# Turning the last row group of block 0 by DMA instead of on TensorE, with a fourth feature computed meanwhile

## The chip, the cores and the metric

The kernel runs on one core of one Trainium2 chip. The metric is the device time of one execution in microseconds (us); the figure before the change is the median of three runs. The profile is of one more execution, whose own time is given beside its span below.

## The reference

The input is x, 2048 rows of 512 features in bf16. The rows are normalised, and two branches of the normalised rows are added to x:

```
xn  = layernorm(x)                                   # over the 512 features
ssm : Bu = xn @ B_bar^T;  h[t] = Lam_bar * h[t-1] + Bu[t]   (complex, 512 states)
      y  = 2 * Re(h @ C^T) + xn * Dskip
glu : out = (silu(xn @ w1) * (xn @ w3)) @ w2         # 1792 hidden features
result = x + y + out
```

B_bar and Lam_bar are made from the small parameters Lambda_re, Lambda_im and log_dt (512 values each).

## The kernel before, in words

The 2048 rows are cut into four blocks of 512 rows, and a block into four row groups of 128 rows (groups 0 to 3). The 1792 hidden features are cut into 14 features of 128 (here a "feature" f is such a group of 128 columns of w1 and w3). TensorE needs the normalised rows turned, with the 512 input features on the partitions: that is the tile `xnT` of a block, 128 partitions by 4 by 512. For feature f of a block, `glu_mm` (L372) adds four matmuls into one PSUM bank for w1 (`g_ps`) and four into another for w3 (`u_ps`), each 128 by 512. ScalarE then takes the bank of w1 through silu (L388, `sl16`) and copies that of w3 (L390, `up16`); VectorE multiplies the two into `hgT` (L397). There are eight PSUM banks.

The order of the work on every engine is the order in which the program text issues it: the schedule is written by hand. Only the side work of VectorE is taken from a queue (`push`, `drain`) between features, in a fixed order.

Blocks 1 to 3 are turned by transposing DMAs that SyncE issues (L232). Block 0, at the start, is turned on TensorE: `turn(c, ...)` issues four 128 by 128 transposes for row group c (L251) into a PSUM tile, and `put` copies them into `xnT` on ScalarE (L256) or VectorE (L258). To keep TensorE at work while the rows arrive and are normalised, `ahead(...)` computes features 0, 1 and 2 on those row groups that are already turned, 128 or 256 rows at a time; their six banks are `begun`. The other two banks hold `xt_a` and `xt_b`, in which the transposes land. The small parameters lie in the tile `prm` and are transposed by one matmul (L544); `par_cols` copies the result out on ScalarE (L271), takes an exponential (L273), and GpSimd makes small columns of them. `glu_up` then runs over all 14 features of block 0; for a feature in `begun` it does only the rows of group 3 (`ts = slice(TBLK - P, TBLK)`).

Around the change, block 0's start runs like this. VectorE normalises group 2 (`normed(2)`, L192); TensorE does half of w3's products for groups 0 and 1, transposes group 2, does the other half, transposes `prm`, and does features 0 for group 2; VectorE has meanwhile copied group 2 (`put(2)`, L258) and normalised group 3 (L192). TensorE then transposes group 3, and does features 1 and 2 of group 2 while VectorE copies group 3 out (L258). ScalarE computes `r_col` (L549), loads the table of silu (L550) and begins with feature 0.

The DMAs of the weights go through SyncE's ring in this order: w1 and w3 for features 0 to 3, then 4 to 7, then the rows of block 1, then w1 and w3 for features 8 to 13 (L95, L117), `dskip_row` (L119), the eight transposing DMAs that load `bt` (L103, for the state-space branch), the rows of block 2, and later the four turns of block 1 (L232). ScalarE's own ring carried only the small parameters and the rows of groups 2 and 3 of block 0, at the very start (L109, L77).

Of the kernel before, what the change touches and what calls it, by code (L numbers as in the profile page):

```python
# [16 lines left out]
P = 128  # L17
# [3 lines left out]
def kernel(  # L21
# [24 lines left out]
    nc = tc.nc  # L46
# [8 lines left out]
    NDT = D // P  # L55
# [14 lines left out]
    def ps_tile(name):  # L70
        return psum.tile([P, 512], FP32, name=name, tag="ps")
# [10 lines left out]
    w1_sb = const.tile([P, NDT, F], BF16, name="w1_sb")  # L82
    w3_sb = const.tile([P, NDT, F], BF16, name="w3_sb")
# [4 lines left out]
    H = NDT // 2  # L88
# [56 lines left out]
    begun = [(ps_tile("g_ps"), ps_tile("u_ps")) for _ in range(3)]  # L145
# [13 lines left out]
    xnTs = [None] * NBLK  # L159
# [28 lines left out]
    def normed(c, parts=1):  # L188
        xn = work.tile([P, D], BF16, name="xn", bufs=8)
        for i in range(parts):  # L190
            ds = slice(i * D // parts, (i + 1) * D // parts)
            nc.vector.tensor_scalar(out=xn[:, ds], in0=x_blk[c // CPB][:, c % CPB, ds], scalar1=mv_all[:, c, 0:1],  # L192
                                    scalar2=rstd_all[:, c:c + 1], op0=ALU.subtract, op1=ALU.mult)
        return xn
# [49 lines left out]
    xt_a = psum.tile([P, 2 * NDT, P], BF16, name="xt_ps", tag="ps")  # L244
    xt_b = psum.tile([P, 2 * NDT, P], BF16, name="xt_ps", tag="ps")
    pprm = xt_a[:, NDT]
    xn0 = xns_of[0] = {}

    def turn(c, pxt, d0=0, d1=NDT):
        for dt in range(d0, d1):  # L250
            nc.tensor.transpose(out=pxt[:, dt - d0, :], in_=xn0[c][:, dt * P:(dt + 1) * P], identity=ident)  # L251

    def put(c, pxt, eng, d0=0, d1=NDT):
        dst = xnTs[0][:, d0:d1, c * P:(c + 1) * P]
        if eng is nc.scalar:
            nc.scalar.activation(out=dst, in_=pxt, func=ACT.Copy)  # L256
        else:
            nc.vector.tensor_copy(out=dst, in_=pxt)  # L258
# [10 lines left out]
    def par_cols():  # L269
        prmc = const.tile([P, 3 * NPT], FP32, name="prmc")  # L270
        nc.scalar.activation(out=prmc, in_=pprm[:, :3 * NPT], func=ACT.Copy)  # L271
        col["lre"], col["lim"], col["ldt"] = (prmc[:, i * NPT:(i + 1) * NPT] for i in range(3))
        nc.scalar.activation(out=c4("dt"), in_=col["ldt"], func=ACT.Exp)  # L273
        nc.gpsimd.tensor_tensor(out=c4("kr"), in0=col["dt"], in1=col["lre"], op=ALU.mult)
        nc.gpsimd.tensor_tensor(out=c4("ki"), in0=col["dt"], in1=col["lim"], op=ALU.mult)
        nc.gpsimd.tensor_scalar(out=c4("turn"), in0=col["ki"], scalar1=float(1.0 / (2.0 * np.pi)), scalar2=None,
                                op0=ALU.mult)
        tt = nc.gpsimd.tensor_tensor
        tt(out=c4("den"), in0=col["lre"], in1=col["lre"], op=ALU.mult)
        tt(out=c4("d2"), in0=col["lim"], in1=col["lim"], op=ALU.mult)  # L280
        tt(out=col["den"], in0=col["den"], in1=col["d2"], op=ALU.add)
# [87 lines left out]
    def glu_mm(b, f, w_sb, ps, ts, dts=range(NDT), joins=False):  # L369

        for dt in dts:
            nc.tensor.matmul(out=ps[:, ts], lhsT=w_sb[:, dt, f * P:(f + 1) * P], rhs=xnTs[b][:, dt, ts],  # L372
                             start=(dt == 0 and not joins), stop=(dt == NDT - 1))
# [128 lines left out]
    def ahead(w_sbs, fs, c, n=1, dts=range(NDT), joins=False):  # L502
        for f in fs:
            for w_sb in w_sbs:
                glu_mm(0, f, w_sb, begun[f][w_sb is w3_sb], slice(c * P, (c + n) * P), dts, joins)

    t1 = [ps[:, :P].bitcast(BF16).rearrange("p (t c) -> p t c", c=P) for ps in begun[2]]
    ta, tb, t2, t3 = xt_a[:, :H], xt_b[:, :H], xt_b[:, NDT:], xt_a[:, :NDT]

    stats(0)  # L510
    aggr(0)
# [19 lines left out]
    B3 = (0, 1, 2)  # L531
    lo, hi = range(H), range(H, NDT)
# [5 lines left out]
    rstd_act(3, 4)  # L538
    ahead((w3_sb,), B3, 0, 2, lo)
    turn(2, t2)  # L540
    put(2, t2, nc.vector)
    xn0[3] = normed(3)
    ahead((w3_sb,), B3, 0, 2, hi)
    nc.tensor.transpose(out=pprm, in_=prm, identity=ident)  # L544
    par_cols()
    ahead((w1_sb, w3_sb), (0,), 2)
    turn(3, t3)
    put(3, t3, nc.vector)
    nc.scalar.activation(out=r_col, in_=col["kr"], func=ACT.Exp)  # L549
    nc.scalar.preload_act_table_set("silu_and_others")  # L550
    ahead((w1_sb, w3_sb), (1, 2), 2)

    push([(3.2, par_turns), (0.2, par_recip)])
    push([(0.0, lambda: for_act.extend(par_trig()))])
# [53 lines left out]
```

## Time and profile before

| what | value |
|---|---|
| median of 3 runs | 211.85 us (211.66 to 211.96) |
| the profiled execution's own time | 212.11 us |
| its span in the profile | 210.3 us |
| TensorE (PE) busy | 206.6 us, 98% of the span |
| VectorE (DVE) busy | 173.5 us, 82% |
| ScalarE (ACT) busy | 93.4 us, 44% |
| granted TensorE clock | 1.0 |
| SyncE's DMA ring (q1) | 13.24 MB |
| ScalarE's DMA ring (q10) | 0.27 MB |

The span runs from the first to the last instruction in the trace; the 1.8 us by which the execution's own time is longer lie outside it. All times below are counted from the start of the span. PEld is TensorE's weight load, which overlaps the matmuls. "SPq" and "ACTq" rows are DMA issues: their length is the time in which the issuing engine's sequencer is taken up, not the time of the transfer.

### The profile page before, as it was taken

The page shows a single profiled execution, that of the slowest core. Times are in us where ns is not written, and L with a number is a line of the kernel's source. Part 1 is how long each engine was busy: PE and PEld are TensorE (multiplying, and loading weights), DVE is VectorE, ACT ScalarE, POOL GpSimd, SP SyncE. Part 2 cuts the span into 40 slices and gives each one's busy share as a digit, 9 for nine tenths or more (in the row PEclk, how much of TensorE's full clock was granted, in tenths as well). Part 3 has the DMA queues.
Part 4 walks back from the last instruction along what each step waited for, and adds up shares of the span by engine and source line. Part 5 has one row for each costly group of instructions (what it writes and reads, how often), then busy time and mean ns, then how long its engine had stood idle before and what let it go on. Part 6 is the DMA issues. An engine that isn't in the chain of part 4 may idle for free.

```text
span 210.3 us, 2878 instructions
## 1 busy us (share of the span) xinstructions
PE 206.6 (98%) x1036; PEld 97.7 (46%) x1036; DVE 173.5 (82%) x346; ACT 93.4 (44%) x167; POOL 6.0 (3%) x27
## 2 busy tenths in 40 slices
PE   8999999999999999999999999999999999999994
PEld 3864444444444444444444444444444444444453
DVE  4699989989999999999999999999999999121111
ACT  3599967666666200066666600036666620000000
POOL 2010320000000000000000000000000000000000
PEclk9999999999999999999999999999999999999999
DMA  5999599944000000000004200100000000000110
GB/s 165 294 366 219 109 178 325 217 106 100 0 3 0 0 25 25 28 26 0 0 0 77 28 1 24 50 25 5 0 0 0 0 3 25 27 25 25 34 44 25
DMA packets 25014, 13.69 MB, mean 65 GB/s; under 512 B 15912, under 2 KB 25000, under 8 KB 25000
## 3 DMA queue, kind: packets, MB, share of 16 engines
q1 hardware_dynamic: 24704, 13.24, 26.1%
q10 hardware_dynamic: 296, 0.27, 0.4%
q8 instruction: 8, 0.13, 0.3%
q14 instruction: 6, 0.05, 0.1%
HBM read 7.74 MB, written 2.10 MB: 47 GB/s over the span
## 4 chain that ended last, share of the span: by engine, by line
PE 96%; DMA 2%; SPq 0%; DVE 0%; issue 0%
PE g_ps L372 23%; PE u_ps L372 23%; PE y_ps L488 23%; PE y_ps L493 13%; PE bu_ps L411 13%; DMA w_sb<-in_B_w_dram 2%; SPq L77 0%; PE xt_ps L251 0%; DVE o L498 0%; PE xt_ps L544 0%
## 5 line engine op out<-in xcount | busy, mean ns | idle before, releaser
L372 PEld LDWEIGHTS <-w_sb 128*128 128x128 bf16 x502 | 46.4, 98 | 50.6 <-DMA w_sb<-in_B_w_dram 0.6
L372 PE MATMUL g_ps<-xnT,w_sb 128*128 128x512 bf16 (+2 forms) x254 | 58.2, 354 | 0.3 <-DMA w_sb<-in_B_w_dram 0.3
L372 PE MATMUL u_ps<-xnT,w_sb 128*128 128x512 bf16 (+2 forms) x248 | 58.4, 358 | 0.0
L488 PE MATMUL y_ps<-w_sb,hgT 128*128 128x512 bf16 (+2 forms) x238 | 51.2, 366 | 0.0
L390 ACT ACTIVATE up<-u_ps 128x512 bf16<-128x512 f32 x56 | 34.0, 607 | 14.9 <-PE u_ps L372 14.9
L413 ACT ACTIVATE u<-bu_ps 128x512 bf16<-128x512 f32 x32 | 19.1, 597 | 46.3 <-PE bu_ps L411 46.3
L388 ACT ACTIVATE sl<-g_ps 128x512 bf16<-128x512 f32 x56 | 34.0, 608 | 9.9 <-PE g_ps L372 9.2
L445 DVE TENSOR_TENSOR_SCAN ab<-r_col,h,ab 128x256 bf16<-128x256 f32 x56 | 37.7, 733 | 0.2
L488 PEld LDWEIGHTS <-hgT 128*128 128x128 bf16 x238 | 22.8, 98 | 25.9
L498 DVE TENSOR_TENSOR o<-y_ps,x_blk 128x512 bf16<-128x512 f32 (+2 forms) x17 | 11.1, 654 | 24.3 <-PE y_ps L493 24.3
L493 PE MATMUL y_ps<-ct,h 128*128 128x512 bf16 (+2 forms) x136 | 30.4, 366 | 0.0
L411 PE MATMUL bu_ps<-xnT,bt 128*128 128x512 bf16 x128 | 28.1, 379 | 0.0
L397 DVE TENSOR_TENSOR hgT<-sl,up 128x512 bf16<-128x512 bf16 x56 | 22.9, 414 | 2.1 <-ACT up L390 2.1
L493 PEld LDWEIGHTS <-h 128*128 128x128 bf16 x136 | 13.0, 98 | 14.7
L411 PEld LDWEIGHTS <-bt 128*128 128x128 bf16 x128 | 12.5, 98 | 15.1
L164 DVE BATCH_NORM_STATS2 stats<-x_blk 128x6 f32<-128x512 bf16 x16 | 10.6, 675 | 2.5 <-DMA x_blk<-in_A_x_dram 2.5
L454 DVE TENSOR_TENSOR ab<-ab,tab_s 128x2048 bf16<-128x2048 bf16 x8 | 9.8, 1222 | 0.2
L450 DVE TENSOR_TENSOR ab<-ab,tab_c 128x2048 bf16<-128x2048 bf16 x8 | 9.8, 1222 | 0.1
L427 DVE TENSOR_TENSOR ab<-u,tab_x 128x2048 bf16<-128x2048 bf16 x8 | 9.7, 1219 | 0.0
L430 DVE TENSOR_TENSOR ab<-u,tab_y 128x2048 bf16<-128x2048 bf16 x8 | 9.7, 1218 | 0.0
L201 DVE TENSOR_TENSOR x_blk<-xd,x_blk 128x512 bf16<-128x512 bf16 x16 | 6.8, 426 | 0.5
L200 DVE TENSOR_TENSOR xd<-xn,dskip_row 128x512 bf16<-128x512 bf16 x16 | 6.7, 418 | 0.0
(76 smaller groups left out, 81.3 us busy)
## 6 DMA issues: line engine op xcount, KB each, us to landing
out_dram<-o SPq DMA_DIRECT2D x15, 128.0 KB, 1.7
w_sb<-in_B_w_dram SPq DMA_DIRECT2D x1, 1792.0 KB, 9.3
x_blk<-in_A_x_dram SPq DMA_DIRECT2D x3, 512.0 KB, 6.3
w_sb<-in_B_w_dram SPq DMA_DIRECT2D x2, 768.0 KB, 7.8
w_sb<-in_B_w_dram SPq DMA_DIRECT2D x4, 256.0 KB, 5.0
w_sb<-in_B_w_dram SPq DMA_DIRECT2D x2, 512.0 KB, 4.1
x_blk<-in_A_x_dram SPq DMA_DIRECT2D x2, 128.0 KB, 2.2
x_blk<-in_A_x_dram ACTq DMA_DIRECT2D x1, 256.0 KB, 4.7
```

Source lines behind the costliest of these rows:

```text
L164: nc.vector.bn_stats(out=sums[c], in_=x_blk[c // CPB][:, c % CPB, :])
L372: nc.tensor.matmul(out=ps[:, ts], lhsT=w_sb[:, dt, f * P:(f + 1) * P], rhs=xnTs[b][:, dt, ts], start=(dt == 0 and not joins), stop=(dt == ...
L388: nc.scalar.activation(out=sl16, in_=g_ps, func=ACT.Silu)
L390: nc.scalar.activation(out=up16, in_=u_ps, func=ACT.Copy)
L397: nc.vector.tensor_tensor(out=hg[b][:, f, :], in0=sl16, in1=up16, op=ALU.mult)
L411: nc.tensor.matmul(out=u_ps, lhsT=bt[ri][:, dt, pt * P:(pt + 1) * P], rhs=xnTs[b][:, dt, :], start=(dt == 0), stop=(dt == NDT - 1))
L413: nc.scalar.activation(out=u16[:, :, pt, ri, :], in_=u_ps.rearrange("p (s t) -> p s t", s=NSB), func=ACT.Copy)
L445: nc.vector.tensor_tensor_scan(out=a[:, pt, 2 * ri + 1, :], data0=r_b, data1=a[:, pt, 2 * ri, :], initial=init, op0=ALU.mult, op1=ALU.add)
L450: nc.vector.tensor_tensor(out=a[:, :, 0::2, :], in0=a[:, :, 1::2, :], in1=tab_b("c"), op=ALU.mult)
L488: nc.tensor.matmul(out=y_ps[:, ds], lhsT=hg[b][:, f, cl * P:(cl + 1) * P], rhs=w2_sb[:, f, ds], start=(f == 0), stop=False)
L493: nc.tensor.matmul(out=y_ps[:, ds], lhsT=h_tiles[i][:, pt, ri, h_ts], rhs=ct[ri][:, pt, ds], start=False, stop=(pt == NPT - 1 and ri == 1))
L498: nc.vector.tensor_tensor(out=o16[:, ds], in0=y_ps[:, ds], in1=x_blk[b][:, cl, ds], op=ALU.add)
```

## The change: a transposing DMA on ScalarE's ring, and feature 3 started early

Group 3 of block 0 is no longer turned on TensorE. After `par_cols`, ScalarE issues one transposing DMA that writes the columns of group 3 into `xnT` straight from the normalised rows in SBUF. The four transposes (L251) and VectorE's copy (L258) of that group are gone. `normed(3)` stands ahead of `put(2)` on VectorE, and the transpose of `prm` and `par_cols` stand ahead of the second half of w3's products. A fourth pair of banks is taken for feature 3 (the banks that held `xt_a` and `xt_b`), and features 0 to 3 are done for groups 0 to 2 before `glu_up` begins.

```diff
-    ta, tb, t2, t3 = xt_a[:, :H], xt_b[:, :H], xt_b[:, NDT:], xt_a[:, :NDT]
+    ta, tb, t2 = xt_a[:, :H], xt_b[:, :H], xt_b[:, NDT:]
...
     turn(2, t2)
+    xn0[3] = normed(3)
     put(2, t2, nc.vector)
-    xn0[3] = normed(3)
-    ahead((w3_sb,), B3, 0, 2, hi)
     nc.tensor.transpose(out=pprm, in_=prm, identity=ident)
     par_cols()
-    ahead((w1_sb, w3_sb), (0,), 2)
-    turn(3, t3)
-    put(3, t3, nc.vector)
+    nc.scalar.dma_start_transpose(out=xnTs[0][:, :, 3 * P:], in_=xn0[3])
+    ahead((w3_sb,), B3, 0, 2, hi)
+    begun.append((ps_tile("g_ps"), ps_tile("u_ps")))
+    ahead((w1_sb,), (3,), 0, 2)
+    ahead((w1_sb, w3_sb), B3, 2)
+    ahead((w3_sb,), (3,), 0, 2)
+    ahead((w1_sb, w3_sb), (3,), 2)
     nc.scalar.activation(out=r_col, in_=col["kr"], func=ACT.Exp)
     nc.scalar.preload_act_table_set("silu_and_others")
-    ahead((w1_sb, w3_sb), (1, 2), 2)
```

In the compiled order of the changed program, the first `bt` DMA on SyncE waits for the new DMA to land, and the first matmul of `glu_up` (feature 0, group 3) waits for it too. The order of all other instructions on the five engines is as before.

## The prediction

> **What bounds the kernel now.** I read the page first: engine totals, then the chain of work that ended last.
>
> ```profile
> PE 206.6 (98%) x1036; PEld 97.7 (46%) x1036; DVE 173.5 (82%) x346; ACT 93.4 (44%) x167; POOL 6.0 (3%) x27
> ...
> PE 96%; DMA 2%; SPq 0%; DVE 0%; issue 0%
> ```
>
> TensorE is the bound. In the timeline its matmuls run back to back from 6.48 us to the end; after 6.48 no start is later than the matmul before it explains. So only two things can change the time: the number of columns TensorE streams, and a new wait of TensorE. Every microsecond of such a wait goes to the end, one for one, because no later gap can absorb it.
>
> Next the timeline around the change, 8 to 12.4 us (start, length, engine, line, operation, tiles).
>
> ```profile
> 8.46 0.20 ACT L172 ACTIVATE rstd_all<-rstd_all 128x1 f32<-128x1 f32 x1
> 8.49 0.39 PE L251 MATMUL xt_ps<-ident,xn 128*128 128x128 bf16 x4
> ...
> 8.72 0.82 PE L372 MATMUL u_ps<-xnT,w_sb 128*128 128x256 bf16 x6
> 8.92 0.42 DVE L258 COPY xnT<-xt_ps 128x512 bf16<-128x512 bf16 x1 [0.73 <-PE xt_ps L251]
> 9.26 0.40 DVE L192 TENSOR_SCALAR xn<-x_blk,mv_all,rstd_all 128x512 bf16<-128x512 bf16 x1
> ...
> 9.37 0.22 PE L544 MATMUL xt_ps<-ident,prm 128*128 128x128 bf16 x1
> ...
> 9.63 0.18 ACT L271 ACTIVATE prmc<-xt_ps 128x12 f32<-128x12 bf16 x1 [0.97 <-PE xt_ps L544]
> ...
> 9.84 0.20 ACT L273 ACTIVATE c_dt<-prmc 128x4 f32<-128x4 f32 x1
> 9.88 0.39 PE L251 MATMUL xt_ps<-ident,xn 128*128 128x128 bf16 x4
> ...
> 10.59 1.28 ACT L550 ACT_TABLE_LOAD   x1
> ...
> 10.84 1.94 SPq L103 DMA_TRANSPOSE bt<-in_A_B_re_dram  x1
> ```
>
> The row of four transposes at 9.88 is what the change removes; the next PE row starts at 10.10, so they cost 0.22 us, 0.056 each. The six 256-row matmuls from 8.72 to 9.37 start 0.109 apart; the 512-row ones from 12.33 on start 0.216 apart.
>
> Last, what a transposing DMA of this very shape takes when the DMA engines are otherwise idle (block 2's turns, 46 to 53 us), and what the rings did. The issue durations are minimum/median/maximum in ns.
>
> ```profile
> L232 SPq DMA_TRANSPOSE xnT<-xn x4: 1212/1216/1221, 46.4 to 50.3; - x4
> ...
> DMA to landing us min/median/max: 2.3/2.3/2.4
> ```
>
> The same kind of issue while the weights were still streaming:
>
> ```profile
> L103 SPq DMA_TRANSPOSE bt<-in_A_B_re_dram x4: 1587/1869/2677, 10.8 to 17.4; - x4
> ```
>
> Rings in three windows: 46 to 53, 9 to 12, and 3.75 to 5 us (packets, MB, share of 16 engines' time).
>
> ```profile
> q1 hardware_dynamic: 2720, 0.66, 41.6%
> ```
> ```profile
> q1 hardware_dynamic: 1120, 1.11, 107.6%
> ```
> ```profile
> q1 hardware_dynamic: 233, 0.23, 54.6%
> q10 hardware_dynamic: 195, 0.19, 42.3%
> ```
>
> The first window is five transposing DMAs: 544 packets each, 34 on each engine, at 0.416 x 16 x 7000 / 2720 = 17 ns. The second is the weights: all 16 engines full, 1.076 x 16 x 3000 / 1120 = 46 ns a packet. The third is the one stretch in which ScalarE's ring and SyncE's ring both had work: they got 195 and 233 packets, close to one for one.
>
> **The change part by part: TensorE's own work.** Removed: 4 transposes x 0.056 = 0.22 us. Feature 3 was 8 matmuls of 512 rows, 8 x 0.216 = 1.73; it is now 8 of 256 and 16 of 128 rows, 8 x 0.109 + 16 x 0.056 = 1.77, so +0.04. Net -0.18 us: the whole possible gain, 0.09% of the time. About 0.2%, here 0.42 us, is what a measurement of this kernel can tell from no change.
>
> **The cover.** After group 2's transposes end their slots at 8.72, TensorE has this to do before it needs group 3: `prm` 0.06; six matmuls of 256 rows, 0.65; four of 256, 0.44; 24 of 128, 1.34; four of 256, 0.44; eight of 128, 0.45. It comes to the waiting matmul at 12.09 us. Its other inputs are in time: `put(2)` moves behind `normed(3)`, to 9.13 to 9.55, and is needed at 9.86; the bank of `xt_a` is read by L271 by 9.16 and needed at 9.43; the weights of feature 3 came with those of features 0 to 2.
>
> **When the DMA is issued.** `normed(3)` needs L172, done at 8.66: with 0.40 it ends at 9.10. The transpose of `prm` comes 0.65 earlier, at 8.72, so L271 runs at 8.98 and L273 at 9.19 to 9.39. The issue stands behind both on ScalarE: about 9.3 (between 9.2, if only L273's dispatch holds it, and 9.4).
>
> **When it lands.** Idle engines: 9.3 + 2.3 = 11.6, half a microsecond inside the cover. But it runs at 10 to 13 us, where the windows show 16 engines full with weights. If its 34 packets on each engine alternate with weight packets, as the two rings did at 3.75 to 5 us, its data takes 34 x (17 + 46) = 2.1 us in place of 34 x 17 = 0.6: 1.55 us more. It lands at 9.3 + 2.3 + 1.55 = 13.15. The trace holds no transposing DMA against another ring's backlog, so both sides are bounded: below by 11.6, above by the slowest `bt` issue, 2.68 in place of 1.21, which adds 1.46 and gives 14.6. I take 13.15, because the window of two rings is the nearest row; the other transfer on ScalarE's ring beside weights, 256 KB of rows, took 4.7 us from issue to landing, which would give 14.0. Start of the waiting matmul: 13.2 with 0.05 from landing to start, as at 6.43 to 6.48. TensorE then stands still for 13.2 - 12.09 = 1.11 us.
>
> The Trainium skill speaks against the move: "VectorE: DVE Perf Modes", section "The three transpose paths", gives 1309 ns for a 128 by 128 block by DMA against 390 ns on TensorE. As an estimate from that page, four such blocks in a row are 5.2 us, a landing at 14.5 and a time of 214.1. The trace differs on both sides: 2.3 us for four blocks in one DMA, 0.056 for one in TensorE's stream.
>
> **What waits behind it.** On ScalarE the issue holds back L549 and the table load (1.28), then silu of feature 0. With 1.2 to 2.7 us of issue the table is in at 12.0 to 13.5; feature 0 is complete at 13.65, so TensorE's wait hides it. Feature 4 needs feature 0's `g_ps` bank back: silu ends at about 14.4, TensorE is there at 15.0. Without TensorE's wait the table is in at 12.0 against 12.5 for feature 0, still hidden. VectorE loses the 0.42 copy, in idle time. On SyncE `dskip_row` (L119) stays ahead, but the first `bt` issue waits for the landing, 10.84 to 13.15, with the rest of SyncE's queue behind it: the other `bt` DMAs, block 2's rows, block 1's turns. At most 2.3 us of delay: the last `bt` landed at 25.6 and is first used at 31.1; block 1's turns landed at 31.3 and are first used at 38.4. The weights of features 4 to 7 had landed by 12.2, and the new packets take 0.6 us of each engine; w3's are used from 14.9 on. All of this costs nothing.
>
> **The sum.** -0.18 + 1.11 = +0.93 us. On the profiled execution, 210.3 + 1.8 around it = 212.11, that is 213.04; on the median, which lies 0.26 lower, 212.8.
>
> **Rivals.** *Covered (0.20).* ScalarE's ring is its own, with nothing ahead of it, and the DMA lands near the idle 2.3 us. It decides at 12.04: earlier, and TensorE never waits and keeps the whole -0.18, 211.67; up to 12.2 it still isn't slower, and up to 12.65 it is within 0.2%. For it: the ring carries nothing else then, and a lull in DMA share (0.69 in 7 to 9 us) lies just before. Against it: 1.07 in 9 to 11 and 1.10 in 11 to 13, and the 4.7 us of ScalarE's other load. "DMA: Bandwidth & Descriptors", section "Issuing engines are not separate DMA queues" in the Trainium skill, says that DMAs of all issuers run on the same 16 engines and interleave; the two rings at 3.75 to 5 us agree.
>
> *Slow issue as well (0.22).* The issue itself is stretched as the `bt` ones were, to 1.6 to 2.7 us, on top of the shared engines: landing at 13.55 to 14.6; with the wait counted as above, 213.2 to 214.2. For it: four of four such issues between 10.8 and 19 were long, and SyncE issues `dskip_row` in 1.31 at that moment. Against it: they went into a ring with its own backlog.
>
> *Blocks in series (0.04).* The four blocks of the DMA go one after another, each with the 1.1 us from end of issue to landing: 1.2 + 4 x 1.1 = 5.6, landing at 14.9, 214.5. The 2.3 us row speaks against it. The Trainium skill's 1309 ns, above, is of this kind.
>
> **How the numbers follow.** Forecast 0.52, and slower with the last two: 0.78. Covered or nearly, within 0.2%: 0.20. Faster by over 0.2%: 0.02, since -0.18 is all there is, and only scatter could add to it. The range goes from 211.6 (covered, with the runs' scatter of 0.1) to 214.3 (the slowest issue, with the same scatter).
>
> **What would show it.** Right: on PE a gap of about 1.1 us before L372's first 128-row matmul of group 3, near 12.1, ended by the DMA `xnT<-xn`; that DMA 3.9 us from issue to landing; ring q10 beside q1 at 10 to 13 us; PE without gaps afterwards; `bt` issues from 13.2. Wrong: no gap there, an issue start far from 9.3, or a later gap of PE that ends on ScalarE, VectorE or `bt`.

## The result: 220.35 us, 4.1% slower; the wait is where it was forecast, six times as long, and the clock falls in it

The changed kernel takes 220.35 us (median of 6 runs, 219.73 to 221.34) against 211.81 (6 runs): a ratio of 1.0408, 95% interval 1.0387 to 1.0429. The profiled execution took 221.01 us, its span 219.2. The forecast was 212.8 with a range of 211.6 to 214.3.

From the page of the changed kernel: engine totals, the granted clock in 40 slices of 5.5 us, and the chain that ended last.

```profile
PE 209.2 (95%) x1048; PEld 100.8 (46%) x1048; DVE 173.7 (79%) x345; ACT 93.9 (43%) x167; POOL 5.6 (3%) x27
...
PEclk9995899999999999999999999999999999999999
...
PE 94%; DMA 4%; DVE 0%; issue 0%
```

TensorE is busy for 95% in place of 98%, a DMA now holds 4% of the chain in place of 2%, and in the fourth slice (16.4 to 21.9 us) only 0.5 of the clock is granted.

The timeline of the changed kernel, 7 to 24 us, in the columns of before:

```profile
8.97 0.20 ACT L273 ACTIVATE c_dt<-prmc 128x4 f32<-128x4 f32 x1
9.04 1.29 ACTq L545 DMA_TRANSPOSE xnT<-xn  x1
...
10.60 1.28 ACT L553 ACT_TABLE_LOAD   x1
...
11.65 0.39 PE L372 MATMUL u_ps<-xnT,w_sb 128*128 128x128 bf16 x4
...
18.54 0.58 PE L372 MATMUL g_ps<-xnT,w_sb 128*128 128x128 bf16 x4 [6.50 <-DMA xnT<-xn]
...
18.58 5.12 SPq L103 DMA_TRANSPOSE bt<-in_A_B_re_dram  x4
...
19.16 0.60 ACT L388 ACTIVATE sl<-g_ps 128x512 bf16<-128x512 f32 x1 [7.28 <-PE g_ps L372]
...
21.91 1.91 PE L372 MATMUL g_ps<-xnT,w_sb 128*128 128x512 bf16 x4
```

The issue starts at 9.04 and is not stretched (1.29). TensorE has used up its cover at 11.88 (four matmuls from 11.65 at 0.056) and stands until 18.54. The landing, from the list of DMA issues, is 9.5 us after the issue, where the forecast had 3.9:

```profile
xnT<-xn ACTq DMA_TRANSPOSE x1, 9.5
```

Then the clock. Busy times in two stretches of the changed kernel (PE, PEld, DVE, ACT, POOL, then the granted clock, DMA share, GB/s):

```profile
18.50:23.80 5.30, 5.26 (x37) 4.12 (x37) 2.96 (x8) 4.53 (x9) 0.00 (x0) 0.50 0.37 89
24.00:40.00 16.00, 16.00 (x76) 7.28 (x75) 13.99 (x48) 13.33 (x24) 2.97 (x13) 1.00 0.73 177
```

For 5.3 us after the gap TensorE streams at half rate: the 512-row matmuls from 21.91 start 0.427 apart in place of 0.216.

The account has four terms. The gap is 6.66 us (11.88 to 18.54). From there to feature 5's start at 24.59 it takes 6.05 us for work that is 1.79 + 1.73 = 3.52 at full clock, so 2.53 more. TensorE came to the gap at 11.88 and not at 12.09, as the timeline of before gives it, so 0.21 less: the first product of block 0 started at 5.97 in place of 6.48, but its first matmuls ran 0.107 apart in place of 0.056, at half rate, until 6.8. And TensorE's own work is 0.18 less. That is 6.66 + 2.53 - 0.21 - 0.18 = 8.80. Feature 5 started at 15.79 before, 8.80 earlier, and the spans differ by 8.9. After 24 us TensorE has no further gap: nothing later takes part.

### The profile page after: what moved, and what is told of

Read it like the earlier page. It is cut to its first block, busy times and chain, and to the rows that moved or that the text cites. A ratio compares the mean times of both kernels' runs of the same rounds, so it can differ in the third digit from the quotient of the medians.

```text
span 219.2 us, 2903 instructions
## 1 busy us (share of the span) xinstructions
PE 209.2 (95%) x1048; PEld 100.8 (46%) x1048; DVE 173.7 (79%) x345; ACT 93.9 (43%) x167; POOL 5.6 (3%) x27
## 4 chain that ended last, share of the span: by engine, by line
PE 94%; DMA 4%; DVE 0%; issue 0%
PE g_ps L372 22%; PE y_ps L488 22%; PE u_ps L372 22%; PE y_ps L493 13%; PE bu_ps L411 13%; DMA xnT<-xn 4%; PE g_ps L150 2%; PE xt_ps L251 0%; DVE xnT L258 0%; DVE o L498 0%; PE g_ps L251 0%; PE u_ps L251 0%
## 5 line engine op out<-in xcount | busy, mean ns | idle before, releaser
L372 PEld LDWEIGHTS <-w_sb 128*128 128x128 bf16 x518 | 49.8, 103 | 56.4 <-issue 7.9
L372 PE MATMUL g_ps<-xnT,w_sb 128*128 128x512 bf16 (+2 forms) x262 | 60.7, 360 | 6.5 <-DMA xnT<-xn 6.5
L372 PE MATMUL u_ps<-xnT,w_sb 128*128 128x512 bf16 (+2 forms) x256 | 59.6, 359 | 0.0
L388 ACT ACTIVATE sl<-g_ps 128x512 bf16<-128x512 f32 x56 | 33.5, 598 | 17.3 <-PE g_ps L372 17.1
L192 DVE TENSOR_SCALAR xn<-x_blk,mv_all,rstd_all 128x512 bf16<-128x512 bf16 (+1 forms) x18 | 6.3, 392 | 0.6 <-ACT rstd_all L172 0.5
```

The source lines that it names most:

```text
L388: nc.scalar.activation(out=sl16, in_=g_ps, func=ACT.Silu)
```

## The experiments

Two theories at first. **A, the 16 shared engines**: the DMA's packets stand behind and between weight packets. **B, ScalarE's ring**: a transposing DMA from there is slow by itself. For the half rate after the gap: the clock falls because TensorE stood still, or the matmuls are slow for another reason.

**Without the DMA.** Feature 3 early as in the change; group 3 turned on TensorE.

```diff
-    nc.scalar.dma_start_transpose(out=xnTs[0][:, :, 3 * P:], in_=xn0[3])
...
+    ahead((w1_sb, w3_sb), (0,), 2)
+    turn(3, t3)
+    put(3, t3, nc.vector)
+    ahead((w1_sb, w3_sb), (1, 2), 2)
     begun.append((ps_tile("g_ps"), ps_tile("u_ps")))
...
```

> Feature 3 started early as in the change, but group 3 is turned on TensorE and copied by VectorE as before; the DMA is gone. Both theories put the whole loss on the wait for the DMA: no gap of TensorE near 12 us, clock 1.0 throughout, and a time within 0.2% of before (the four transposes are back, and feature 3's narrower matmuls add 8 x 0.109 + 16 x 0.056 - 8 x 0.216 = 0.04 us): 211.7 to 212.1. If the early feature itself costs something (its two banks, its place in the order), it is above 212.3.

Measured: 211.78 us, ratio 0.9995 (0.9985 to 1.0004). The other half of the change costs nothing and brings nothing that can be told; the loss came with the DMA.

**The gap filled with work.** The last piece of the cover is done 16 times.

```diff
-    ahead((w1_sb, w3_sb), (3,), 2)
+    for _ in range(16):
+        ahead((w1_sb, w3_sb), (3,), 2)
```

> The changed kernel, with the last eight 128-row matmuls before the wait (feature 3, group 2) done 16 times over in place of once: 15 x 0.45 = 6.7 us of work that only repeats a result, put into the gap. Theory of the clock: the gap lets the granted clock fall to 0.5 from 17.0 to 23.8 us of the span, and the 5.3 us of matmuls that ran in it would have taken half, so 2.65 us come back: the clock stays at 1.0, the DMA lands at 18.5 as it did, and the time is 217.5 to 218.0. Rival: the slow matmuls after the gap come from something else (operands, contention), and the time stays at 220.3.

Measured: 218.59 us (218.48 to 218.9), ratio 1.0321 (1.0305 to 1.0336) against the change's 1.0408. The DMA landed at 18.48, as in the change; the clock never fell. The same stretch after the landing, same columns:

```profile
18.60:22.00 3.40, 3.35 (x40) 2.49 (x40) 1.39 (x4) 3.06 (x7) 0.00 (x0) 1.00 0.37 96
```

So the half rate was the clock, and it followed from TensorE standing still. The clock is worth 220.35 - 218.59 = 1.8 us between the medians, less than expected, and 2.5 between the two profiled spans (219.2 and 216.7); the change's profiled execution is one of its longer ones. How far the length of the gap varies between executions is not known.

**No queue ahead of the DMA and none beside it.** On SyncE's ring all that follows w1 of features 4 to 7 waits for the landing, by a copy that reads the result.

```diff
+    load_one(w1_sb, w1v, 4, 8)
...
     nc.scalar.dma_start_transpose(out=xnTs[0][:, :, 3 * P:], in_=xn0[3])
+    gate = const.tile([P, 16], BF16, name="gate")
+    nc.sync.dma_start(out=gate, in_=xnTs[0][:, 0, 3 * P:3 * P + 16])
+    load_one(w3_sb, w3v, 4, 8)
+    ...
```

> The changed kernel, but on SyncE's ring everything behind w1 of features 4 to 7 is held back by a small copy that reads the turned rows, until the transposing DMA has landed. So at its issue no weight transfer is queued. Theory A (16 shared engines: the DMA waits for the weight packets queued before it, alternates with those behind, and all its 16 engines move together): 2.3 to 2.6 us from issue to landing, no gap of TensorE at group 3; the weights come later, so perhaps a gap of up to 2 us at feature 4 or 8: 211.7 to 214. Theory B (a transposing DMA from ScalarE's ring is slow by itself, whatever else runs): landing 9 us after issue as before, 219 to 222.

Measured: 213.92 us in the profiled run; a second run, without a profile, took 217.39 at a mean clock of 0.992, and what held it can't be seen, so only the profiled run is read here. The DMA issues of ScalarE and SyncE in the timeline of this kernel:

```profile
8.79 1.29 ACTq L543 DMA_TRANSPOSE xnT<-xn  x1
11.36 0.55 SPq L545 DMA_DIRECT2D gate<-xnT  x1
```

The copy, which waits for the landing, goes out 2.57 us after the issue. TensorE's waits in this kernel show none for the DMA, only one at feature 4, for the weights that were held back:

```profile
PE u_ps L370 <- DMA w_sb<-in_B_w_dram: 2.1, 1, 2.1
```

Theory B falls, as far as one profiled run goes: from ScalarE's ring, too, this DMA takes about 2.5 us when the engines are free.

**On SyncE's ring, ahead of the other weights.** The same order of loads, the DMA issued by SyncE.

```diff
-    nc.scalar.dma_start_transpose(out=xnTs[0][:, :, 3 * P:], in_=xn0[3])
+    nc.sync.dma_start_transpose(out=xnTs[0][:, :, 3 * P:], in_=xn0[3])
+    load_one(w3_sb, w3v, 4, 8)
+    ...
```

> The transposing DMA is issued by SyncE on its own ring, ahead of w3 of features 4 to 7 and all that follows; ScalarE issues nothing. Theory A: behind it on the ring only w1 of features 4 to 7 was queued, so it lands 2.3 to 3.2 us after an issue at about 9.0; TensorE waits 0 to 0.4 us, the clock stays at 1.0: 211.5 to 212.2. Theory B (ScalarE's ring is the fault) gives the same here, so that this run is of use with the one above; if the transposing DMA is slow on either ring at this time, the time is above 215.

Measured: 212.2 us, ratio 1.0016 (1.0004 to 1.0027). The DMA landed 2.45 us after its issue, ahead of TensorE; w3 of features 4 to 7, now behind it, came at 15.07, and TensorE stood 0.83 us for it. The row of the matmul names another releaser; the weight load beside it names the DMA:

```profile
15.11 0.98 PEld L370 LDWEIGHTS <-w_sb 128*128 128x128 bf16 x6 [1.16 <-DMA w_sb<-in_B_w_dram]
```

The wait moved from one load to the next. It hung on a single engine: the trace notes sixteen arrivals for each of these DMAs, as many as there are engines, and for w3 fifteen of them had come by 14.09, before TensorE was ready at 14.28; the sixteenth came at 15.07. The transposing DMA's sixteen had all come between 10.96 and 11.13. Between 11.07 and 12.59 one engine has a 16 KB record of the ring that the profile calls `instruction` (q8), and from then on the last arrival of each load is about a microsecond behind the others. The trace does not number the engines, so that it is the one with the record is inferred.

**The same, with the loads cut by features.** Ahead of the DMA w1 and w3 of features 4 and 5, behind it those of 6 and 7.

```diff
+    load_w13(4, 6)
...
+    nc.sync.dma_start_transpose(out=xnTs[0][:, :, 3 * P:], in_=xn0[3])
+    load_w13(6, 8)
+    ...
```

> The transposing DMA on SyncE's ring as before, but the weights of features 4 and 5, of w1 and of w3, stand ahead of it (the same 512 KB), and those of 6 and 7 behind it. Theory A: it lands about 2.5 us after its issue, at 11.1 to 11.4, ahead of the 11.85 at which TensorE needs it; w3 of feature 4 is there in time, and those of 6 and 7 land by 15, needed at 17.2: no gap of TensorE after 6.5 us, and the whole 0.18 us of the forecast's sum are kept: 211.5 to 211.8, ratio 0.998 to 1.000. If the later weights are late, up to 212.3.

Measured: 211.8 us, ratio 1.0007 (0.9996 to 1.0018). The transposing DMA in this kernel, and all the waits that TensorE has left (it is the start of the kernel):

```profile
L539 SPq DMA_TRANSPOSE xnT<-xn x1: 1304/1304/1304, 8.4 to 8.4; - x1
...
DMA to landing us min/median/max: 2.4/2.4/2.4
```
```profile
PE g_ps L144 <- PEq L595: 0.8, 1, 0.8
```

So group 3 can be turned by DMA at no cost, from 8.4 to 10.8 us, within the cover. The 0.18 us that this saves on TensorE can't be told in the time: no version here beats the kernel before.

**Half the queue.** That an earlier queue matters was shown; these runs ask how. A1 says that an engine first serves what it already holds of the first ring, A2 that turns are taken from the start and that SyncE's issues of the later weights made the delay. Here features 4 to 7 and block 1's rows stay ahead of the DMA, and only what follows is held back until it has landed.

```diff
     load_w13(4, 8)
     nc.sync.dma_start(out=x_blk[1], in_=xv[:, 1, :, :])
...
+    nc.sync.dma_start(out=gate, in_=xnTs[0][:, 0, 3 * P:3 * P + 16])
+    load_w13(8, NFT)
+    ...
```

> The changed kernel, but w1 and w3 of features 8 to 13 and dskip_row are held back on SyncE's ring until the transposing DMA has landed; w1 and w3 of features 4 to 7 and block 1's rows stay ahead of it. At its issue (9.0) about 1.1 MB is still queued, which runs to about 13.2. Theory A1 (an engine serves the other ring only after what it already holds of the first, some 64 packets each): the first packet of the DMA comes at about 13 as before, and with nothing behind it the data takes 0.9 us and no turn-taking: landing 14.2 to 14.6, a gap of TensorE of 2.4 to 2.8 us. Theory A2 (rings take turns from the start; the delay to 13.3 came from SyncE's issues of the later weights, which were held up because their ring was full): first packet at 10.2 to 10.5, landing 12.5 to 13, gap 0.7 to 1.2 us. The time adds a possible later wait for the held-back weights of feature 8.

Measured: landing 4.9 us after an issue at 8.84, the gap 2.1 us, 213.74 in the profiled run (a second one, without a profile, took 215.37 at a mean clock of 0.992, which would fit a gap that was long enough there for the clock to fall). Rings in two windows of this kernel, 10 to 11.7 and 11.7 to 13.1 us (packets, MB, share):

```profile
q1 hardware_dynamic: 600, 0.60, 109.8%
```
```profile
q10 hardware_dynamic: 544, 0.13, 62.2%
q1 hardware_dynamic: 107, 0.09, 21.2%
```

Not one packet of ScalarE's ring in the first window, all 544 in the second, when SyncE's queue has run down to its last 107. The first packet came at 11.72, earlier than A1 said because the queue ended earlier, and later than A2's 10.2. The queue goes first; turns are not taken from the start. Whether the DMA's packets stood at the engines by then or came there late, the trace does not show.

Two such windows of the changed kernel, before and after the first packet (9 to 13.3, and 13.3 to 17.9 us):

```profile
q1 hardware_dynamic: 1424, 1.58, 108.0%
```
```profile
q1 hardware_dynamic: 647, 0.97, 87.3%
q10 hardware_dynamic: 544, 0.13, 17.5%
q8 instruction: 1, 0.02, 1.9%
```

On free engines the first packet comes 1.2 to 1.3 us after the issue (1.20 in block 2's turns of before, 1.26 in the run with no queue). Counted from 1.2 us after the issue, the weights were served alone from 10.2 to 13.3: 952 packets of mostly 1 to 1.5 KB, some 60 for each of the 16 engines on average. In the run with the filled gap it was 64, and 60 in the run with a plain copy below. After that the rings take turns, packet by packet.

**Turns only.** SyncE's ring is held back only until the rows are normalised, so that the weights start beside the DMA, with nothing queued before. The cut is against the kernel with no queue ahead.

```diff
-    nc.sync.dma_start(out=gate, in_=xnTs[0][:, 0, 3 * P:3 * P + 16])
+    nc.sync.dma_start(out=gate, in_=xn0[3][:, 0:16])
```

> The changed kernel, but on SyncE's ring everything behind w1 of features 4 to 7 is held back only until group 3's rows are normalised (a small copy that reads them), so that the weights start together with the transposing DMA, with no queue ahead of it. Theory A1: first packet 1.1 us after issue, at about 10, then turns with weight packets, 34 x (17 + 46) = 2.1 us of data in place of 0.6: landing at 12.3 to 13; if one of the 16 KB instruction records falls into the data, 1.4 us more, as all 16 engines stand still with it. Theory A2 gives the same start. If turn-taking costs nothing, landing 11.3 to 11.6.

Measured: 216.3 us (215.89 and 216.71), landing 6.2 us after the issue, beyond what was expected. The first packet came at 10.17, 1.3 us after the issue, as on free engines. The weights' first packets came only at 10.7, when 372 of the 512 data packets were through, so that turns are seen for the last 140 alone. Rings from 10.1 to 11.7 and from 11.7 to 14 us:

```profile
q10 hardware_dynamic: 512, 0.13, 45.2%
...
q1 hardware_dynamic: 115, 0.12, 37.0%
```
```profile
q1 hardware_dynamic: 798, 0.80, 103.4%
...
q8 instruction: 1, 0.02, 2.7%
...
q10 hardware_dynamic: 32, 0.00, 0.8%
```

The 512 data packets are through in 1.4 us (0.8 on free engines). Only the 32 small packets that report the end, two for each engine, come late, at 12.6 to 13.7, the last two on the heels of a 16 KB instruction record that ran from 12.7 to 13.7. Fifteen of the sixteen arrivals had come by 13.75, and the last came at 15.04, which is the landing. So here the end of the DMA was late though its data was not: a microsecond on all engines, and 1.3 us more on one. Why the reports wait a microsecond when nothing of the DMA is left was not found. The gap here was 3.4 us, and the clock fell in both runs (0.992).

**A plain copy in its place.** TensorE turns group 3; ScalarE issues a copy of the same rows in 512 pieces of 256 bytes, which nobody waits for.

```diff
...
-    nc.scalar.dma_start_transpose(out=xnTs[0][:, :, 3 * P:], in_=xn0[3])
+    plain = const.tile([P, NDT, 2 * P], BF16, name="plain")
+    nc.scalar.dma_start(out=plain[:, :, 0:P], in_=xn0[3].rearrange("p (t c) -> p t c", c=P))
...
```

> Group 3 is turned on TensorE, as in the run with feature 3 early; at the place of the transposing DMA ScalarE issues a plain copy of the same rows into an unused tile, in the same 512 pieces of 256 bytes, under the same full queue of weights. Nobody waits for it, so the time is that of before, 211.6 to 212. What counts is its packets on ScalarE's ring. If the late start belongs to the queue and not to transposing, they begin at about 13.3 as well; if the standstill of all engines belongs to transposing, these packets and the weights show no hole of 1.4 us near the 16 KB instruction record, and the copy is in by 15.5 to 16 in place of 18.5. If the late start belongs to transposing, the copy's packets begin at 10.2 to 10.5.

Measured: 211.87 us, ratio 1.0002 (0.9992 to 1.0012). The first packet came at 13.34, as in the change: the late start belongs to the queue, not to transposing. The landing was expected at 15.5 to 16, and is as late as that of the transposing DMA:

```profile
plain<-xn ACTq DMA_DIRECT2D x1, 128.0 KB, 9.6
```

By the end reports, 14 of the 16 engines were through by 16.3, one at 16.7 and one at 18.2; a landing is that of the last engine. The transposing DMA's sixteen arrivals in the change all came between 18.38 and 18.50. What differs is the rest of the traffic. Both kernels have a 16 KB instruction record on one engine, from 14.15 to 15.51 in the change and from 14.24 to 15.34 here. Stretches at that record, columns as before: before, the change, the plain copy.

```profile
14.90:16.30 1.40, 1.40 (x8) 0.67 (x7) 1.40 (x5) 1.40 (x5) 0.00 (x0) 1.00 1.02 366
```
```profile
14.90:16.30 1.40, 0.00 (x0) 0.00 (x0) 0.00 (x0) 0.00 (x0) 0.00 (x0) 1.00 0.94 28
```
```profile
14.20:15.40 1.20, 1.20 (x8) 0.49 (x7) 0.78 (x3) 1.20 (x3) 0.00 (x0) 1.00 1.10 345
```

With the transposing DMA in progress the engines are held (0.94) but move only 28 GB/s: 13 packets of weights each last 1.2 to 1.5 us. With the plain copy, or without either, the traffic goes on at 345 to 366. The run with the filled gap, where the transposing DMA met a record from 14.72 to 15.77, shows the same:

```profile
15.30:16.40 1.10, 1.10 (x24) 1.10 (x22) 0.00 (x0) 0.00 (x0) 0.00 (x0) 1.00 0.36 13
```

In block 1's turns by DMA the longest packet lasts 1.41 to 1.52 us in the six traces where such a record falls in, and 0.52 to 1.10 in the four where none does. This fits transposing as work that all 16 engines do in step, so that one held engine holds all. It is read from traces with and without the record; the record itself was not moved on purpose.

## Why the prediction was wrong, point by point

*What bounds the kernel; a wait goes to the end one for one.* Right. Every microsecond of the gap is in the time, and TensorE has no later gap.

*TensorE's own work, -0.18 us.* The account by the trace closes with it; in the times it is too small to be seen, also in the version by DMA without a wait (1.0007).

*The cover and the issue.* Right: cover to 11.88 (forecast 12.09; block 0's products began earlier), issue at 9.04 (9.3), 1.29 us long. ScalarE's queue, the bank of feature 0 and SyncE's `bt` DMAs were hidden as reasoned: `bt` began at 18.58, 7.7 us later than before, and TensorE never waited for it.

*When it lands: 13.15.* This step failed, at 18.50. It had 2.3 us plus 1.55 for taking turns, and three terms were missing or too small. First, the start: I took the two rings at 3.75 to 5 us as the pattern, but there SyncE's queue was short. From 3 to 3.75 us, with ScalarE's load already running, SyncE's ring moved 22 packets:

```profile
q10 hardware_dynamic: 49, 0.05, 42.1%
q1 hardware_dynamic: 22, 0.02, 10.3%
```

With a full queue the first packet came at 13.3, 4.3 us after the issue in place of 1.2: 3.1 us. Second, the data, 13.3 to 17.7: 4.4 us against the 2.1 that the forecast gave it, 1.4 of the difference in the standstill. Third, the report of the end: 0.8 us from the last data packet, 0.5 on free engines. With the issue 0.26 earlier than forecast that makes the 5.35 us between 13.15 and 18.50. Two rows of before would have warned. `dskip_row`, a load of the same size issued at nearly the same moment behind the same weights, but on SyncE's own ring, landed 9.6 us after its issue:

```profile
dskip_row<-in_A_Dskip_dram SPq DMA_DIRECT2D x1, 128.0 KB, 9.6
```

And its issue took 1.31 us, which I used only for the length of ScalarE's issue; with the loads held back it took 0.50 (half the queue) and 0.67 (no queue), so its length was a sign of a full queue.

*The upper bound, 14.6.* It was taken from the slowest issue. The bound that was needed was the queue: the last weights issued ahead of the DMA's place landed at 18.7 in the trace of before, and nothing in that trace put the DMA ahead of them.

*The clock.* Not in the sum at all, since a gap of 1.1 us did not call for it. It was worth 1.8 to 2.5 us. The Trainium skill, "TensorE: Matmul & The Clock Gate", section "Why this matters for your kernels", says that a gap of over about 3 us between matmuls takes the clock back to half. The traces agree: the clock fell with gaps of 6.66 and 3.4 us, and did not with gaps of 2.1 us (half the queue, and no queue).

*The rivals.* "Slow issue as well" and "blocks in series" had the direction, by mechanisms that are not seen: the issue was of normal length, and four blocks took 2.4 us in one DMA. "Covered" is what happens on free engines. In the Trainium skill, "DMA: Bandwidth & Descriptors", section "Queues, rings and completion order", each engine takes turns between the rings that it has work for, a packet at a time. The trace agrees only from 13.3 us on; that some 60 packets an engine were served first does not follow from that rule.

## What to carry to other kernels

A short DMA on the critical path should be priced by what is already queued on the engines when it is issued, also on another ring: here 2.5 us on free engines, 4.9 behind a short queue, 9.5 behind a long one. A load of the same size in that queue shows how long it is. If it must be there, hold back or reorder the bulk loads around it, and then look which load has become the late one. And a long wait of TensorE has a second price, the clock after it: 3.4 us of gap had it here, 2.1 us had not.

## What the runs showed of the hardware that I had not expected

- A second ring is no way past a full first one: some 60 packets an engine (3.1 us) were served before the first of the other ring, for a transposing DMA and for a plain copy alike.
- While a transposing DMA was in progress, a 16 KB instruction record on one engine went with a standstill of all traffic: 28 GB/s over 1.4 us, against 345 to 366 with a plain copy or with neither. The run with the filled gap shows the same (13 GB/s over 1.1 us).
- With nothing queued ahead and weights starting 0.5 us behind its first packet, the DMA had its data through in 1.4 us and was still reported only 6.2 us after its issue.
- After a 16 KB instruction record, one of the sixteen arrivals of each load came about a microsecond behind the others, and a landing counts all sixteen: the 0.83 us wait with the DMA on SyncE's ring was for that last one.
